# Step 1's pieces placed one step behind the blocks of full-float32 products

## The chip, the cores and the metric

The kernel runs on one core of one Trainium2 chip. Its time is the device time of one execution, in microseconds. Before the change three runs took 1006.72, 1007.61 and 1007.96 us, median 1007.61. The profile is one further execution.

The engines are PE (matrix products), PEld (the loading of its stationary operand), ACT, DVE and POOL (elementwise work) and SP, which issues nearly all DMAs. Each engine does its instructions in program order and waits on semaphores for the others.

## The reference

```python
X = np.fft.fft(x, axis=1)           # x: 8 x 3136 x 256
X = np.fft.fft(X, axis=2)
x = X.real.astype(np.float32)
mu = np.mean(x, axis=-1, keepdims=True)
var = np.mean((x - mu) ** 2, axis=-1, keepdims=True)
xn = (x - mu) / np.sqrt(var + 1e-06) * g_ln
ch = np.maximum(xn @ w_ch1, 0.0) @ w_ch2
return x + ch
```

A two-dimensional Fourier transform of each of eight batches, of which the real part is kept, then a layer norm, a two-layer network with ReLU (256 to 1024 to 256), and a residual sum.

## The kernel before, in words

**The Fourier transform along the sequence** is done in two steps, 3136 = 64 x 49. Step 1 is a transform of length 64, step 2 one of length 49 with the twiddles in its table. Only half of the tokens (1567 a batch, `REG`, and two single ones) go through the network's first product, since the others are their mirror images; the transform along the 256 features is folded into the first weights and, for the residual, into a table `ty_s`.

**Chunks and steps.** The tokens of all batches stand in 49 chunks of 256. The main loop runs over steps s; step s works on chunk s // 8 and on 128 of the 1024 inner features. In a step, PE does six products in `moe1_a` (L354, into a PSUM tile `ab`, two buffers) and, for the step three before, twelve in `moe2` (L404, into `acc`). They are float32 numbers split in a high and a low part, three passes for each product. ACT copies half of `ab` to `asb` (L359), DVE makes `h` of it (L360, L361), ACT rounds `h` to `h_hi` (L368) and DVE makes `h_lo` (L369). `moe1_b(s - 1)` comes ahead of `moe1_a(s)`, so on ACT and DVE h_hi and h_lo of a step stand ahead of asb and h of the next.

**Further work** is put into two lists by step: `late` (after `moe1_a`) and `after` (at the end of the step). The order within each engine is the order in which the program writes it.

- *Blocks.* At steps 5 mod 8 `step2` (L309, products in full float32, one or two groups of tokens; a step with two is called a double block here) and `residual` (L428, also full float32) make one block on PE. ACT copies the results at the same step (L330, L332), DVE makes the low part `ckl` one step later (L334). `residual_e` (ACT) and `residual_y` (DVE, L442 to L455) follow one to three steps behind, `std` (ACT, L460) at steps 1 mod 8, `inverse_std` (DVE, L467 to L471: a reciprocal and three small operations) at steps 2 mod 8, and `finish` (L477, L479) at 3 and 4 mod 8. For the first group of a batch, `step2` adds a product with `zmu` (L313).
- *Step 1's pieces.* Each batch has seven, `step1(b, i)`: three products of 512 columns (L262) at the end of a step d, into PSUM tile `y` (one buffer), which the second group of a double block uses too; ACT copies the result into `s1` (L265) and SP stores it (`store1`, L269). Ahead of it, POOL folds the input, `fold_zw` at d - 7 (L207, L208) and `fold_eo` at d - 6 (L213, L214), ACT rounds the fold, `fold_hi` at d - 4 (L219), and POOL makes its low part, `fold_lo` at d - 3 (L225). `load_x` of the next batch stands at d - 5. POOL does these in their order as soon as their data and buffers are there, so it often runs ahead of the steps.
- *Edge products.* `ends` (POOL, L190, L194) and `step1_ends` (PE, L237 to L241, then two copies on ACT, the second into the last column of `zmu`).
- *Relayout.* Two steps behind the last piece, SP reads the stored result back in another order (`relayout`, L276) for `step2`.

A batch b needs its relayout at step `need` = 8 * (b * REG // CW) - 3, the step of its block with the zmu product. These are the steps 45, 93, 141, 189, 237, 285 and 333 for batches 1 to 7. The pieces of batches 2 to 7 stand at need - 45, - 42, - 37, - 34, - 29, - 26 and - 21, so at 0 or 3 mod 8, and `fold_hi` at 4 or 7 mod 8.

Of the kernel before, what the change touches and what calls it, by code (L numbers as in the profile page):

```python
# [20 lines left out]
F32 = mybir.dt.float32  # L21
# [7 lines left out]
NB, N, D, FF = 8, 3136, 256, 1024  # L29
NV = 25  # L30
HALF = N // 2 + 1
REG = HALF - 2
CW = 256
# [9 lines left out]
KP = 8 * NS  # L43
# [103 lines left out]
def tile_kernel(ctx: ExitStack, tc: tile.TileContext, x, g_ln, w1, w2, tu, tab, tz, ty, tw, out):  # L147
    nc = tc.nc
    moving = ctx.enter_context(tc.tile_pool(name="moving", bufs=1))
    weights = ctx.enter_context(tc.tile_pool(name="weights", bufs=1))  # L150
    const = ctx.enter_context(tc.tile_pool(name="const", bufs=1))
# [14 lines left out]
    tz_s = const.tile([KP, 50], F32, name="tz_s")  # L166
# [3 lines left out]
    ty_s = const.tile([128, 2, 130], F32, name="ty_s")  # L170
    g_s = const.tile([128, 2], F32, name="g_s")
    xs = const.tile([128, NU, 4, D], F32, name="xs")
    zmu = const.tile([KP, 128], F32, name="zmu")
    masked = const.tile([128, KP], F32, name="masked")
    one = const.tile([128, 1], F32, name="one")
    neg = const.tile([128, 1], F32, name="neg")
# [51 lines left out]
    def alloc1(b):  # L228
        if b not in s1:
            s1[b] = work.tile([128, NS, 2, 128], F32, tag="s1", name=f"s1_{b}", bufs=1)  # L230
            scratch[b] = dram.tile([NS, 128, D], F32, tag="scratch", name=f"scratch{b}")

    def step1_ends(b, p0=0, p1=NS):
        alloc1(b)
        n = p1 - p0
        ps = psum.tile([128, 3, n], F32, tag="y" if b else "fft", name=f"pse{p0}_{b}")
        nc.tensor.matmul(ps[:, 0], tu_s[:, 0:128], e0c[b][:, p0:p1, 1], start=True, stop=True)  # L237
        nc.tensor.matmul(ps[:, 1], tu_s[:, 256:384], e0c[b][:, p0:p1, 0], start=False, stop=True,
                         skip_group_check=True)
        if p1 == NS:  # L240
            nc.tensor.matmul(ps[:KP, 2, 0:1], masked, one, start=False, stop=True,  # L241
                             skip_group_check=True)
        nc.scalar.copy(s1[b][:, p0:p1, :, 127], ps[:, 0:2].rearrange("p h s -> p s h"))
        if p1 == NS:
            nc.scalar.copy(zmu[:, 127:128], ps[:KP, 2, 0:1])

    def step1(b, i):
        alloc1(b)
# [36 lines left out]
    def first_token(m):  # L285
        b, j = divmod(m, 8)
        return b * REG + max(gb[2 * j] - 2, 0)
# [11 lines left out]
    def step2(m, part, of=None):  # L299

        b, j = divmod(m, 8)
        base, end = gb[2 * j], gb[2 * j + 2]
        if "m" in part:
            ps2[m] = psum.tile([128, 2, CW], F32, tag="y" if m in second else "fft", name=f"ps2_{m}")
        ps = ps2[m]
        for g in (2 * j, 2 * j + 1) if "m" in part else ():
            k0, k1 = gb[g], gb[g + 1]
            for h in range(2):
                nc.tensor.matmul(ps[:, h, k0 - base:k1 - base], s2[b][:KP, g, 128 * h:128 * h + 128],  # L309
                                 tab_s[:, h, k0:k1], start=(h == 0 and g == 2 * j), stop=True,  # L310
                                 skip_group_check=True)
            if g == 0:
                nc.tensor.matmul(ps[:, 1, 0:50], zmu, tz_s, start=False, stop=True,  # L313
                                 skip_group_check=True)
        if j == 0 and "f" in part:
            nc.scalar.copy(single[:, :, 2 * b:2 * b + 2], ps[:, :, 0:2])
        t, stop = first_token(m), b * REG + end - 2
        while t < stop:
            c = t // CW
            n = min(stop, c * CW + CW) - t  # L320
            if c not in chunk:
                parts = (weights.tile([128, 2, CKW - 32], F32, tag="ck", name=f"ck{c}", bufs=3),
                         moving.tile([128, 2, CKW], F32R, tag="ck_hi", name=f"ckh{c}", bufs=3),
                         moving.tile([128, 2, CKW], F32R, tag="ck_lo", name=f"ckl{c}", bufs=3))
                chunk[c] = tuple(p[:, :, :MAXW] for p in parts)
            full, hi, lo = (x[:, :, t - c * CW:t - c * CW + n] for x in chunk[c])
            p0 = t - b * REG + 2 - base
            src = ps[:, :, p0:p0 + n]
            if "h" in part and of in (None, c):
                nc.scalar.copy(hi, src)  # L330
            if "f" in part:
                nc.scalar.copy(full, src)  # L332
            if "l" in part and of in (None, c):
                nc.vector.tensor_tensor(out=lo, in0=src, in1=hi.bitcast(F32), op=ALU.subtract)  # L334
            t += n
# [272 lines left out]
    def add(s, fn, *args):  # L608

        after.setdefault(s, []).append((fn, args))  # L610

    def add_late(s, fn, *args):

        late.setdefault(s, []).append((fn, args))

    first = {}
    for m in range(3, 64):
        s = 8 * (first_token(m) // CW) - 3
# [3 lines left out]
    for s, ms in first.items():  # L622
        for m in ms:
            add(s, step2, m, "mhf")
        for m in ms:
            add_late(s + 1, step2, m, "l")
    for b in range(1, NB):
        need = 8 * (b * REG // CW) - 3
        at = [need - d for d in ((45, 42, 37, 34, 29, 26, 21) if b > 1 else
                                 (28, 25, 22, 19, 17, 14, 11))]  # L630
        ends_at = need - (46 if b > 1 else 30)
        add(ends_at - 7, ends, b)
        add(ends_at, step1_ends, b)
        for i, d in enumerate(at):
            d0, d = d, d - (b == 1)
            add(d - 7, fold_zw, b, i, nc.gpsimd)
            if b + 1 < NB:
                add(d - 5, load_x, b + 1, i)
            add(d - 6, fold_eo, b, i)
            add(d - 4, fold_hi, b, i)  # L640
            add(d - 3, fold_lo, b, i)
            add(d0, step1, b, i)
            add(d0, store1, b, i)
        add(at[-1] + 2, relayout, b)
    for c in range(LC):
        s = 8 * c + (5 if c > 1 else 6)
# [26 lines left out]
    with tc.manual_schedule(engines={E.PE, E.Activation, E.DVE, E.Pool}):  # L673
        with tc.manual_schedule(engines={E.SP}):
# [33 lines left out]
            nc.sync.dma_start(tab_s[:, :, :gb[4]], tab[:, :, :gb[4]])  # L708
            nc.sync.dma_start(tz_s, tz)
            step1_ends(0, 0, 6)  # L710
            for i in range(3):
                store1(0, i, nc.scalar if i % 2 else nc.gpsimd)
# [5 lines left out]
            step1(0, 4)  # L718
            finish_w1(0)
            step1_ends(0, 6, 10)  # L720
            store1(0, 3, nc.scalar)
            store1(0, 4, nc.gpsimd)
# [46 lines left out]
            convert_b("w2_1")  # L769
            warm_up(15, warm_h)  # L770
            step2(0, "m")
            step2(0, "hl")
            step2(1, "m")
# [72 lines left out]
```

## Time and profile before

| | |
|---|---|
| median of the three runs | 1007.61 us |
| the profiled execution | 1007.27 us |
| its span, from the first to the last instruction | 1005.5 us |
| PE's granted clock, mean | 1.000 |
| products L404 | 3 x 1568, mean 279 ns |
| products L354 | 3 x 768, mean 279 to 286 ns |
| pieces' products L262 | three for each of 49 pieces |
| copies L265 | 56, mean 585 ns |

PE's products are pipelined: each lasts 279 ns in the trace, and the next starts 113 to 118 ns behind it. The time of a product on PE is therefore read from start to start, not from its duration.

In the rows of a timeline the first column is the start in us from the span's start, the second the duration in us; behind a form in square brackets stand the engine's idle time before the instruction and what ended it. In the rows of waits stand the total in us, the number of times and the longest. In the rows of windows stand the window, its length, the busy time of the engine with the number of instructions that touch it, the granted clock, the DMA's busy share and GB/s.

The chain of work that ended last has PE for 88% of the span (L404 49%, L354 25%), DVE for 7% and ACT for 2%.

### The profile page before, as it was taken

To read this page: it belongs to the slowest core of one execution; us is meant where nothing else is said; L and a number is where in the kernel's file an instruction comes from. 1 tells how busy PE (TensorE), PEld (TensorE's weight loads), DVE (VectorE), ACT (ScalarE), POOL (GpSimd) and SP (SyncE) were. 2 spreads that over 40 slices of the span, in tenths; PEclk is the share of its full clock that TensorE was granted. 3 is DMA by queue.
4 is the path that set the end of the run, shared out by engine and by line. 5 is a ranking of instruction groups with operands and counts; after the bars stand their busy time and mean duration, and the time that the engine had idled before them with its cause. 6 is when DMAs were issued, how large, how long until landed. Compare 5 with 4: busy or idle time off the path is not lost.

```text
span 1005.5 us, 21770 instructions
## 1 busy us (share of the span) xinstructions
PE 995.1 (99%) x8289; PEld 973.7 (97%) x8289; DVE 812.3 (81%) x2190; ACT 540.1 (54%) x1416; POOL 243.9 (24%) x278
## 2 busy tenths in 40 slices
PE   9999999999999999999999999999999999999998
PEld 6799999999999999999999999999999999999998
DVE  7788887878787788878877887878788788887887
ACT  3655556554555555655456555555555554555553
POOL 2146414530153203440054401532034300000000
PEclk9999999999999999999999999999999999999999
DMA  9933243223122511333132232224101230100101
GB/s 346 266 141 126 85 143 110 86 84 108 62 95 85 157 44 53 103 120 105 44 111 101 74 106 75 84 96 126 55 32 44 74 105 23 43 22 22 43 22 43
DMA packets 41528, 92.10 MB, mean 92 GB/s; under 512 B 4176, under 2 KB 18704, under 8 KB 40528
## 3 DMA queue, kind: packets, MB, share of 16 engines
q1 hardware_dynamic: 40016, 88.87, 27.1%
q8 instruction: 66, 1.08, 0.5%
q0 software_dynamic: 320, 1.05, 0.3%
q10 hardware_dynamic: 1088, 0.79, 0.2%
q14 instruction: 38, 0.31, 0.1%
HBM read 50.32 MB, written 40.37 MB: 90 GB/s over the span
## 4 chain that ended last, share of the span: by engine, by line
PE 88%; DVE 7%; ACT 2%; DMA 2%; issue 1%; SPq 0%; ACTq 0%; DVEq 0%
PE acc L404 49%; PE ab L354 25%; PE ps L309 5%; PE psy L428 4%; PE ps L262 3%; DVE h_lo L369 2%; DVE h L360 1%; DVE h L361 1%; ACT h_hi L368 1%; PE ps L255 1%; PE ps L257 1%; DMA scratch<-s 1%; DMA s<-scratch 1%; DMA xs<-x 0%; DVE st L450 0%
## 5 line engine op out<-in xcount | busy, mean ns | idle before, releaser
L404 PE MATMUL acc<-w_hi,h_lo 128*128 128x256 f32 x1568 | 437.1, 279 | 0.2 <-DVE h_lo L369 0.2
L404 PE MATMUL acc<-w_hi,h_hi 128*128 128x256 f32 x1568 | 436.9, 279 | 0.0
L404 PE MATMUL acc<-w_lo,h_hi 128*128 128x256 f32 x1568 | 436.9, 279 | 0.0
L369 DVE SCALAR_TENSOR_TENSOR h_lo<-h,h_hi 128x512 fp32r<-128x512 f32 x392 | 285.9, 729 | 160.8 <-ACT h_hi L368 159.0
L368 ACT ACTIVATE h_hi<-h 128x512 fp32r<-128x512 f32 x392 | 250.1, 638 | 266.0 <-DVE h L361 265.5
L404 PEld LDWEIGHTS acc<-w_hi,h_hi 128*128 128x128 f32 x1568 | 296.7, 189 | 0.0
L404 PEld LDWEIGHTS acc<-w_lo,h_hi 128*128 128x128 f32 x1568 | 295.3, 188 | 0.0
L404 PEld LDWEIGHTS acc<-w_hi,h_lo 128*128 128x128 f32 x1568 | 294.6, 188 | 0.6 <-DVE h_lo L369 0.4
L354 PE MATMUL ab<-ckl,w_hi 128*128 128x256 f32 x768 | 219.9, 286 | 2.6 <-DVE h L361 2.5
L354 PE MATMUL ab<-ckh,w_lo 128*128 128x256 f32 x768 | 214.5, 279 | 0.5 <-ACT ckh L330 0.3
L354 PE MATMUL ab<-ckh,w_hi 128*128 128x256 f32 x768 | 214.1, 279 | 0.0
L225 POOL TENSOR_TENSOR fl<-f,fh 128x512 fp32r<-128x512 f32 x49 | 64.2, 1309 | 495.5 <-ACT fh L219 489.3
L360 DVE TENSOR_TENSOR h<-asb,ab 128x256 f32<-128x256 f32 x384 | 158.7, 413 | 1.5 <-ACT asb L359 1.5
L361 DVE TENSOR_TENSOR h<-asb,ab 128x256 f32<-128x256 f32 x384 | 158.8, 414 | 0.0
L354 PEld LDWEIGHTS ab<-ckl,w_hi 128*128 128x128 f32 x768 | 144.3, 188 | 6.5 <-issue 2.1
L359 ACT COPY asb<-ab 128x256 f32<-128x256 f32 x384 | 139.0, 362 | 17.6 <-PE ab L354 13.9
L354 PEld LDWEIGHTS ab<-ckh,w_lo 128*128 128x128 f32 x768 | 144.7, 188 | 3.1 <-ACT ckh L330 0.5
L354 PEld LDWEIGHTS ab<-ckh,w_hi 128*128 128x128 f32 x768 | 145.3, 189 | 0.0
L330 ACT CAST ckh<-ps 128x392 fp32r<-128x392 f32 (+49 forms) x112 | 39.8, 356 | 62.3 <-PE ps L309 62.1
L265 ACT COPY s<-ps 128x508 f32<-128x508 f32 x56 | 32.8, 585 | 71.9 <-PE ps L262 58.7
L309 PE MATMUL ps<-tab_s,s 112*128 112x98 f32 (+1 forms) x512 | 65.6, 273 | 0.6 <-DMA s<-scratch 0.6
L309 PEld LDWEIGHTS ps<-tab_s,s 112*128 112x128 f32 x512 | 61.9, 191 | 1.1 <-PE pw L670 1.1
(108 smaller groups left out, 964.8 us busy)
## 6 DMA issues: line engine op xcount, KB each, us to landing
xs<-x SPq DMA_DIRECT2D x56, 512.0 KB, 4.4
out<-o SPq DMA_DIRECT2D x96, 256.0 KB, 3.0
scratch<-s SPq DMA_DIRECT2D x49, 256.0 KB, 2.2
s<-scratch SPq DMA_DIRECT2D x7, 1792.0 KB, 9.7
w1p_all<-w SPq DMA_DIRECT2D x8, 512.0 KB, 8.7
scratch<-s POOLq DMA_DIRECT2D x4, 256.0 KB, 6.3
s<-scratch SPq DMA_DIRECT2D x2, 448.0 KB, 5.8
s<-scratch SPq DMA_DIRECT2D x1, 896.0 KB, 12.2
```

The costliest lines, as they stand in the source:

```text
L225: nc.gpsimd.tensor_tensor(out=lo, in0=f, in1=hi.bitcast(F32), op=ALU.subtract)
L265: nc.scalar.copy(s[:, :, :, :127], ps[:, :, :, :127])
L309: nc.tensor.matmul(ps[:, h, k0 - base:k1 - base], s2[b][:KP, g, 128 * h:128 * h + 128], tab_s[:, h, k0:k1], start=(h == 0 and g == 2 * j), ...
L330: nc.scalar.copy(hi, src)
L354: nc.tensor.matmul(pt, wt[wi][:, j, fs], ch[xi][:, j, :w], start=(n == 0), stop=(n == 2))
L359: nc.scalar.copy(asb[:, :w], pa)
L360: nc.vector.tensor_tensor(out=h[:, :w], in0=asb[:, :w], in1=pb, op=ALU.add)
L361: nc.vector.tensor_tensor(out=h[:, w:], in0=asb[:, :m], in1=pb[:, :m], op=ALU.subtract)
L368: nc.scalar.activation(h_hi, h, AF.Relu)
L369: nc.vector.scalar_tensor_tensor(out=h_lo, in0=h, scalar=0.0, in1=h_hi.bitcast(F32), op0=ALU.max, op1=ALU.subtract)
L404: nc.tensor.matmul(acc[c, i][:, side], hs[xi][:, h0:h0 + 128], ws[wi][:, f], start=(f == 0 and side == 0 and n == 0), stop=(f == 7 and n = ...
L428: nc.tensor.matmul(ps[:, j, :129 + j], ck[:, j], ty_s[:, j, :129 + j], start=(j == 0), stop=True, skip_group_check=True)
```

## The change

Batch 1 keeps its steps. For batches 2 to 7:

- Five of the seven pieces stand behind the blocks at need - 56, - 40, - 32, - 24 and - 16: one step behind a single block (6 mod 8), two behind a double one (7 mod 8). The other two stand in neighbouring steps, need - 46 and need - 45, behind the block with the zmu product of the batch before. What belongs to a piece (folds, loads, store) keeps its distance to it.
- The relayout keeps its two steps behind the last piece, so it comes at need - 13 or need - 12 instead of need - 19.
- `step1_ends` stands at need - 58 instead of need - 46, `ends` at need - 62 instead of need - 53.
- As the edge products of a batch now come before the zmu product of the batch ahead of it, `zmu` has two columns' worth, one for even and one for odd batches.

```diff
-    zmu = const.tile([KP, 128], F32, name="zmu")
+    zmu = const.tile([KP, 2, 128], F32, name="zmu")
...
-            nc.scalar.copy(zmu[:, 127:128], ps[:KP, 2, 0:1])
+            nc.scalar.copy(zmu[:, b % 2, 127:128], ps[:KP, 2, 0:1])
...
-                nc.tensor.matmul(ps[:, 1, 0:50], zmu, tz_s, start=False, stop=True,
+                nc.tensor.matmul(ps[:, 1, 0:50], zmu[:, b % 2], tz_s, start=False, stop=True,
...
+    def behind(s):
+
+        return s + 1 + (len(first[s]) > 1)
+
+    steps1 = {1: [17, 20, 23, 26, 28, 31, 34]}
+    for b in range(2, NB):
+        need = 8 * (b * REG // CW) - 3
+        steps1[b] = sorted([need - 46, need - 45] +
+                           [behind(need - d) for d in (56, 40, 32, 24, 16)])
     for b in range(1, NB):
         need = 8 * (b * REG // CW) - 3
-        at = [need - d for d in ((45, 42, 37, 34, 29, 26, 21) if b > 1 else
-                                 (28, 25, 22, 19, 17, 14, 11))]
-        ends_at = need - (46 if b > 1 else 30)
-        add(ends_at - 7, ends, b)
+        at = steps1[b]
+        ends_at = need - (58 if b > 1 else 30)
+        add(need - 62 if b > 1 else ends_at - 7, ends, b)
         add(ends_at, step1_ends, b)
```

`first[s]` is the list of the groups that `step2` does at step s; a double block has two.

## The prediction

> **What bounds the kernel now.** I read the page first, then the waits of PE, then PE's busy time in chosen stretches, last the timelines of single engines.
>
> ```profile
> PE 995.1 (99%) x8289; PEld 973.7 (97%) x8289; DVE 812.3 (81%) x2190; ACT 540.1 (54%) x1416; POOL 243.9 (24%) x278
> ```
> ```profile
> PE ab L354 <- DVE h L361: 2.5, 5, 0.8
> ...
> PE ps L262 <- DVE ckl L334: 1.1, 1, 1.1
> ```
>
> PE is busy for 99% of the span and hardly waits: the two rows (us, times, longest) are the only waits of the main loop that matter here. So time can go only where PE's products become quicker, and can come only from a wait that isn't there yet.
>
> Products do have two speeds. Five stretches (length, PE busy, instructions that touch it, granted clock): two of eight steps each, from the first product behind a block of full-float32 products to the next block; then three single steps.
>
> ```profile
> 469.85:486.89 17.04, 17.04 (x147) 1.00 0.06 21
> 488.60:505.02 16.42, 16.42 (x148) 1.00 0.10 36
> 414.39:416.51 2.12, 2.12 (x20) 1.00 0.00 0
> 421.30:423.34 2.04, 2.04 (x20) 1.00 0.00 0
> 424.04:426.16 2.12, 2.12 (x20) 1.00 0.19 65
> ```
> ```profile
> 416.51 0.39 PE L262 MATMUL ps<-fl,t_hi 128*128 128x512 f32 x1
> ...
> 423.34 0.39 PE L262 MATMUL ps<-fl,t_hi 128*128 128x512 f32 x1
> ```
>
> The same 144 products (18 a step) take 17.04 or 16.42 us, at the same full clock: a slow pace of 2.12 us a step and a fast one of 2.04, 0.62 / 8 = 0.078 apart. A pace holds until something other than L354 and L404 runs on PE. The last three rows stand around step 1's pieces (L262) at 416.51 and 423.34: a piece turns slow to fast, the next turns fast to slow. A block entered at the fast pace leaves the slow one; the block with the zmu product, and the edge products, leave the fast one. By these turns 24 of the 48 steps of a batch are slow now.
>
> **The change, part by part.**
>
> *Pace.* From batch 2 on a piece stands at the end of the first step behind a block (of the second, if the block is double), so a block's slow pace lasts one or two steps; the pair behind the zmu block has one slow step between. Per batch: five blocks without zmu, two of them double, and the pair: 5 + 2 + 1 = 8 slow steps. 16 of 48 turn fast; with the ends of the run 98 steps over six batches: 98 x 0.078 = **-7.6 us**. Products are neither added nor removed; batch 1 keeps its steps.
>
> *What a piece behind a block does to ACT and DVE.* Steps 5 mod 8 end with the block. After one, at the fast pace and without a piece, it goes today as follows (first products of steps 6, 3 and 4; then ACT; then DVE):
>
> ```profile
> 370.42 0.37 PE L354 MATMUL ab<-ckl,w_hi 128*128 128x256 f32 x1
> ...
> 380.72 0.28 PE L354 MATMUL ab<-ckl,w_hi 128*128 128x256 f32 x1
> ...
> 382.76 0.28 PE L354 MATMUL ab<-ckl,w_hi 128*128 128x256 f32 x1
> ```
> ```profile
> 372.73 0.63 ACT L368 ACTIVATE h_hi<-h 128x512 fp32r<-128x512 f32 x1
> ...
> 379.64 0.63 ACT L368 ACTIVATE h_hi<-h 128x512 fp32r<-128x512 f32 x1 [1.05 <-DVE h L361]
> 380.17 0.35 ACT L359 COPY asb<-ab 128x256 f32<-128x256 f32 x1
> ```
> ```profile
> 379.19 0.41 DVE L361 TENSOR_TENSOR h<-asb,ab 128x256 f32<-128x256 f32 x1
> ...
> 381.24 0.41 DVE L361 TENSOR_TENSOR h<-asb,ab 128x256 f32<-128x256 f32 x1
> 381.57 0.16 DVE L467 RECIPROCAL ve<-ve 128x2 f32<-128x2 f32 x1
> 381.76 0.16 DVE L468 SCALAR_TENSOR_TENSOR ve<-ve 128x2 f32<-128x2 f32 x1
> ```
>
> Step s+2 needs the PSUM buffer that DVE frees with h of step s. h of step 1 ends at 379.60, step 3 starts at 380.72: 1.12 us to spare; one step on 382.76 - 381.65 = 1.11. DVE's round (h, ACT's h_hi, h_lo, h) takes 381.24 - 379.19 = 2.05 us, no less than PE's fast step: what is lost there isn't won back before the next block.
>
> A piece's copy L265 stands on ACT ahead of the next h_hi:
>
> ```profile
> 437.12 0.28 PE L354 MATMUL ab<-ckl,w_hi 128*128 128x256 f32 x1
> ```
> ```profile
> 437.32 0.58 ACT L265 COPY s<-ps 128x508 f32<-128x508 f32 x1 [1.74 <-PE ps L262]
> 437.80 0.64 ACT L368 ACTIVATE h_hi<-h 128x512 fp32r<-128x512 f32 x1
> ```
>
> It starts 0.20 after the next step's first product, h_hi 0.48 later. With the piece at the end of step 6 (2.20 for that step, 0.70 for the piece: 417.21 less 416.51 in the same timeline), h_hi of step 6 starts 2.90 + 0.68 = 3.58 us after the step does, instead of 372.73 - 370.42 = 2.31. DVE is 1.27 late, PE 0.76. To spare at step 2: 1.11 - 1.27 + 0.76 = **0.60 us**. The same working gives 0.89 behind a double block (piece a step later, while DVE does its y work) and 1.38 behind the zmu block with its two pieces. No wait of PE by itself.
>
> *Where a piece's fold falls.* fold_hi is four steps ahead of the piece. For a piece at 6 mod 8 that is step 2; POOL's fold_lo follows at once, and zw and f of the next piece back to back. Just then DVE does inverse_std (L467 to L471): in the rows above fold_hi would start near 380.44, behind asb, POOL near 381.15 for 1.3 us, and L468 comes at 381.76. Batch 1 has this meeting now (POOL; DVE; PE):
>
> ```profile
> 105.57 1.30 POOL L225 TENSOR_TENSOR fl<-f,fh 128x512 fp32r<-128x512 f32 x1 [2.17 <-ACT fh L219]
> 106.83 0.73 POOL L213 TENSOR_TENSOR f<-zw 128x256 f32<-128x256 f32 x1
> 107.52 0.74 POOL L214 TENSOR_TENSOR f<-zw 128x256 f32<-128x256 f32 x1
> ```
> ```profile
> 105.20 0.41 DVE L361 TENSOR_TENSOR h<-asb,ab 128x256 f32<-128x256 f32 x1
> 105.53 0.16 DVE L467 RECIPROCAL ve<-ve 128x2 f32<-128x2 f32 x1
> 105.72 1.16 DVE L468 SCALAR_TENSOR_TENSOR ve<-ve 128x2 f32<-128x2 f32 x1
> 106.92 0.66 DVE L469 TENSOR_TENSOR ve<-ve 128x2 f32<-128x2 f32 x1
> 107.61 0.66 DVE L471 SCALAR_TENSOR_TENSOR r<-ve 128x2 f32<-128x2 f32 x1
> ...
> 109.13 0.41 DVE L361 TENSOR_TENSOR h<-asb,ab 128x256 f32<-128x256 f32 x1
> ```
> ```profile
> 109.68 0.36 PE L354 MATMUL ab<-ckl,w_hi 128*128 128x256 f32 x1 [0.63 <-DVE h L361]
> ```
>
> L468, L469 and L471 each end when a POOL operation does. From h to h 109.13 - 105.20 = 3.93 us pass instead of 2.05, 1.88 are lost, and PE waits until 0.14 after h. In the new places no L265 stands ahead of fold_hi, so POOL starts 0.48 earlier against DVE and L468 waits 0.5 less; but POOL's run goes on and reaches h_lo, which took 1.07 instead of 0.69 in such a place:
>
> ```profile
> 400.35 1.07 DVE L369 SCALAR_TENSOR_TENSOR h_lo<-h,h_hi 128x512 fp32r<-128x512 f32 x1 [0.70 <-ACT h_hi L368]
> ```
>
> Loss per meeting: 1.88 - 0.48 + 0.38 = 1.78; PE waits 1.78 - (spare - 0.15): 1.33, 1.04 or 0.55. The plan has 15 meetings, fold_hi at steps 58, 82, 114, 162, 298 behind single blocks, 106, 130, 154, 178, 210, 258 behind double ones, 50, 194, 242, 290 behind zmu blocks (a batch's last piece is left out: there POOL must first wait for x, and only fold_lo meets DVE): 6.65 + 6.24 + 2.20 = 15.1 us.
>
> The Trainium skill, page "SBUF — State Buffer", section "Who interferes with whom", speaks against the new places: a DVE instruction with two SBUF inputs and a GpSimd instruction that reads SBUF exclude each other for a whole instruction, one with at most one SBUF input doesn't contend. The rows agree (L360 and L361, which read PSUM, keep 0.41). By it h_lo could be held for a whole 0.74 operation, 15 x 0.36 = 5.4 us more than my sum.
>
> *The edge products* move to step 3 mod 8, in three of these cycles (82, 130, 178) between the meeting and PE's wait:
>
> ```profile
> 392.95 0.29 PE L237 MATMUL pse<-e0c,tu_s 128*128 128x14 f32 x2
> ...
> 393.51 0.36 PE L354 MATMUL ab<-ckl,w_hi 128*128 128x256 f32 x1
> ```
>
> They take 0.56 of PE's time here as there, but in these cycles that shortens the wait: 3 x 0.56 off, **+13.4 us** for the meetings. Bounds: 0, if POOL and DVE miss each other, to 15 x 1.88 = 28, with nothing to spare.
>
> *The rest, together.* The second zmu column costs nothing in the loop: ACT writes one column as before. The loads, stores and the relayout keep their order on SP; the relayout still has twelve steps, some 25 us, before the zmu block reads it; were that too little, PE would wait there. At a double block a piece takes the buffer y of the second product block, two steps behind it; that place is where the 1.1 us row comes from, in batch 1, where DVE was late. At 0 to 1.1 for eleven such pieces, 0 to 12 us, I take 0, since outside batch 1 DVE has no such delay ahead of it.
>
> Sum against the profiled execution of 1007.3 us: 1007.3 - 7.6 + 13.4 = 1013.1; the median of the runs is 0.3 above it: **1013.4 us**.
>
> **The rivals.**
> - *The pace alone: faster.* The meetings cost nothing, because the offset of fold_lo against inverse_std is another, or because there is more than 1.9 us to spare (from there on a meeting is free). For it: the spare is a difference of larger numbers. Against it: the offset is fixed by the chain h, h_hi, asb, fold_hi. 1007.6 - 7.6 = 1000.0, to 1004 with some waits. 25%.
> - *They cancel.* Half the price of the meetings: 1007.6 - 7.6 + 7 = 1007. 10%.
> - *The pace isn't turned there.* A piece one step behind a block, or a zmu block reached in another way, leaves the pace slow; the meetings stay: 1007.6 + 13.4 = 1021. Against it: pieces two steps behind a block turned it. 7%. The Trainium skill, page "TensorE: Matmul & The Clock Gate", section "Wait — 56ns, not 53.3ns?", has one warm start-to-start time, N / 2.4 plus about 2.5 ns, 109 ns for 256 columns, and so no second pace to win; this trace has two, 2.04 / 18 = 113 ns and 2.12 / 18 = 118 ns.
>
> **How the numbers follow.** The forecast has 58%, with 1008 to 1021 as its own range; with the faster rival the range is 998.5 to 1021. About 0.2%, 2 us, is what a measurement of this kernel can tell from no change. Slower: 58 + 7 less 3 for the forecast's low edge, 62%; faster 25 + 2 of the cancelling case, 27%; same 11%.
>
> **What would show it.** Waits of PE for h L361 at about 15 steps 5 mod 8, near 1 us each, with L468 to L471 long beside L225: the meetings are right. L468 at 0.16 throughout and no such wait: they are wrong, and the time is near 1000. Steps behind the pieces at 2.12: the turns are wrong.

## The result: slower by a fifth of a per cent, less than half of what was forecast

| | before | after |
|---|---|---|
| median | 1007.34 us (20 runs, 1006.43 to 1009.52) | 1009.85 us (20 runs, 1007.63 to 1011.55) |
| profiled execution, its span | 1007.27, 1005.5 us | 1010.0, 1008.2 us |

The ratio is 1.0021, with an interval of 1.0014 to 1.0028: slower by 2.5 us. The forecast was 1013.4 us, slower by 5.8 than the 1007.6 known then; the measured time lies in the forecast's own range of 1008 to 1021.

**The page of the changed kernel**, busy time, share of the span and instructions of each engine:

```profile
PE 993.7 (99%) x8289; PEld 969.7 (96%) x8289; DVE 833.4 (83%) x2190; ACT 534.6 (53%) x1416; POOL 240.2 (24%) x278
```

DVE is busy for 21 us more with the same instructions: something makes them longer. PE's busy time fell by 1.4 us while the span grew by 2.7, so PE now stands still for longer. The waits of PE (us in total, times, longest):

```profile
PE ab L354 <- DVE h L361: 6.4, 13, 0.8
...
PE ps L262 <- DVE ckl L334: 1.2, 1, 1.2
```

Before, the first row had five waits and 2.5 us, all ahead of step 35; the other eight are new. DVE's groups (busy us, mean ns), `inverse_std`'s three small operations first, then one of them before the change:

```profile
L468 DVE SCALAR_TENSOR_TENSOR ve<-ve 128x2 f32<-128x2 f32 (+1 forms) x49 | 19.1, 389 | 1.7
L469 DVE TENSOR_TENSOR ve<-ve 128x2 f32<-128x2 f32 (+1 forms) x49 | 16.4, 334 | 1.7
L471 DVE SCALAR_TENSOR_TENSOR r<-ve 128x2 f32<-128x2 f32 (+1 forms) x49 | 14.8, 303 | 1.7
```
```profile
L468 DVE SCALAR_TENSOR_TENSOR ve<-ve 128x2 f32<-128x2 f32 (+1 forms) x49 | 9.3, 189 | 1.7
```

So the meetings with POOL are there: L468 takes twice as long on average. The third thing to look at is the pace. Two stretches of 126 products each, from behind a piece to the next block, as windows of the changed kernel (length, PE busy, instructions that touch it, clock, DMA share, GB/s):

```profile
197.87:212.16 14.29, 14.29 (x127) 1.00 0.21 74
454.06:468.90 14.84, 14.84 (x127) 1.00 0.22 71
```

The first is what the change was to give, 113 ns a product. The second stands behind a piece of the same kind and is slow all the same, at 118.

**The account.** From step 35 to eight steps before the end, all products L354 and L404 of a trace were sorted by the time to the next such product: up to 115 ns is fast (mean 113.3), 116 to 122 slow (mean 117.8). What a longer one exceeds 115 ns by is counted as waiting; the start of a block's followers is kept apart.

| | stretch, us | fast | slow | waiting, us |
|---|---|---|---|---|
| before | 851.98 | 2887 | 3251 | 0.0 |
| after | 854.46 | 4029 | 2080 | 7.1 |

1171 products left the slow pace: 1171 x 4.4 ns = -5.2 us. The waiting is +7.1 us. (The view has 4.2 us in eight waits there. It begins a wait at the last product's end, 0.28 us behind its start, where the next product was due after 0.113; it has no waits shorter than that difference; and the second product behind a wait is late too, some 0.193 us behind the first.) The rest, +0.6, lies in and around the blocks; 0.4 of it is at the residual products (L428) of step 37. The sum, +2.5 us, is the result.

### The profile page after: what moved, and what is told of

It is laid out like the page before. It is cut to its first block, busy times and chain, and to the rows that moved or that the text cites. A ratio compares the mean times of both kernels' runs of the same rounds, so it can differ in the third digit from the quotient of the medians.

```text
span 1008.2 us, 21760 instructions
## 1 busy us (share of the span) xinstructions
PE 993.7 (99%) x8289; PEld 969.7 (96%) x8289; DVE 833.4 (83%) x2190; ACT 534.6 (53%) x1416; POOL 240.2 (24%) x278
## 4 chain that ended last, share of the span: by engine, by line
PE 80%; DVE 13%; ACT 3%; DMA 2%; issue 2%; SPq 0%; ACTq 0%; DVEq 0%
PE acc L404 43%; PE ab L354 22%; PE ps L309 5%; DVE h_lo L369 4%; PE psy L428 4%; PE ps L262 3%; DVE h L361 2%; DVE h L360 2%; ACT h_hi L368 2%; DVE st L450 1%; DVE ve L468 1%; DVE ve L469 1%; DMA scratch<-s 1%; ACT s L265 1%; PE ps L255 1%
## 5 line engine op out<-in xcount | busy, mean ns | idle before, releaser
L404 PE MATMUL acc<-w_hi,h_lo 128*128 128x256 f32 x1568 | 435.7, 278 | 0.1
L404 PE MATMUL acc<-w_lo,h_hi 128*128 128x256 f32 x1568 | 435.5, 278 | 0.0
L404 PE MATMUL acc<-w_hi,h_hi 128*128 128x256 f32 x1568 | 435.5, 278 | 0.0
L368 ACT ACTIVATE h_hi<-h 128x512 fp32r<-128x512 f32 x392 | 249.7, 637 | 322.2 <-DVE h L361 322.1
L404 PEld LDWEIGHTS acc<-w_hi,h_hi 128*128 128x128 f32 x1568 | 295.6, 189 | 0.0
L404 PEld LDWEIGHTS acc<-w_lo,h_hi 128*128 128x128 f32 x1568 | 295.1, 188 | 0.0
L404 PEld LDWEIGHTS acc<-w_hi,h_lo 128*128 128x128 f32 x1568 | 294.6, 188 | 0.4 <-DVE h_lo L369 0.3
L354 PE MATMUL ab<-ckl,w_hi 128*128 128x256 f32 x768 | 220.4, 287 | 6.5 <-DVE h L361 6.4
L354 PE MATMUL ab<-ckh,w_lo 128*128 128x256 f32 x768 | 213.9, 278 | 0.5 <-ACT ckh L330 0.4
L354 PE MATMUL ab<-ckh,w_hi 128*128 128x256 f32 x768 | 213.4, 278 | 0.0
L225 POOL TENSOR_TENSOR fl<-f,fh 128x512 fp32r<-128x512 f32 x49 | 64.1, 1307 | 527.1 <-ACT fh L219 478.4
L354 PEld LDWEIGHTS ab<-ckl,w_hi 128*128 128x128 f32 x768 | 144.3, 188 | 12.5 <-issue 7.6
L354 PEld LDWEIGHTS ab<-ckh,w_lo 128*128 128x128 f32 x768 | 144.7, 188 | 3.1 <-ACT ckh L330 0.5
L354 PEld LDWEIGHTS ab<-ckh,w_hi 128*128 128x128 f32 x768 | 144.8, 189 | 0.0
L359 ACT COPY asb<-ab 128x256 f32<-128x256 f32 x384 | 138.2, 360 | 10.8 <-PE ab L354 9.2
L265 ACT COPY s<-ps 128x508 f32<-128x508 f32 x56 | 32.8, 585 | 64.3 <-PE ps L262 50.5
```

Source lines behind the costliest of these rows:

```text
L225: nc.gpsimd.tensor_tensor(out=lo, in0=f, in1=hi.bitcast(F32), op=ALU.subtract)
L265: nc.scalar.copy(s[:, :, :, :127], ps[:, :, :, :127])
L354: nc.tensor.matmul(pt, wt[wi][:, j, fs], ch[xi][:, j, :w], start=(n == 0), stop=(n == 2))
L359: nc.scalar.copy(asb[:, :w], pa)
L368: nc.scalar.activation(h_hi, h, AF.Relu)
L404: nc.tensor.matmul(acc[c, i][:, side], hs[xi][:, h0:h0 + 128], ws[wi][:, f], start=(f == 0 and side == 0 and n == 0), stop=(f == 7 and n = ...
```

## The experiments

Each was run beside the kernel before on the same chip; that kernel's median was 1007.25 for the first four, 1007.93 for the next three and 1007.48 for the last two. Three theories were at stake: that the waits come from the meetings of POOL with `inverse_std`; that it takes the piece's copy L265 ahead of h_hi as well; and that the pace is what the pieces' places were to win.

**1. The changed kernel without its meetings.** For pieces at 6 mod 8 both folds come one step later.

```diff
-            add(d - 4, fold_hi, b, i)
-            add(d - 3, fold_lo, b, i)
+            later = b > 1 and d % 8 == 6
+            add(d - 4 + later, fold_hi, b, i)
+            add(d - 3 + later, fold_lo, b, i)
```

> The changed kernel, with fold_hi and fold_lo of the pieces at steps 6 mod 8 (batches 2 to 7) one step later, so that POOL's fold_lo no longer runs beside DVE's inverse_std; nothing else moves. Theory A (the meeting of the two makes PE's waits, and the waits also upset the pace): L468, L469 and L471 fall back to 0.16 us in the loop, PE's waits for h fall from 6.4 us (13) to the 2.5 us (5) of the kernel of before, the slow products behind step 35 fall from 2080 to about 1460, and the time is 7.6 us below the kernel of before: about 0.9925 of it. Rival B (the spare of 0.6 us is the cause, and any run of POOL or ACT work at that place uses it up): waits stay near 6 us, ratio 1.00 to 1.002. Rival C (the pace isn't turned reliably in the new places, waits or not): waits go, but slow products stay near 2000, ratio about 0.996.

Measured: 1001.91 us, ratio 0.9943 [0.9931, 0.9956]; the stretch 846.05 us, 1621 slow products, no waiting for h. Its timelines around one `inverse_std` (DVE, then POOL; start, duration):

```profile
324.74 0.16 DVE L467 RECIPROCAL ve<-ve 128x2 f32<-128x2 f32 x1
324.93 0.16 DVE L468 SCALAR_TENSOR_TENSOR ve<-ve 128x2 f32<-128x2 f32 x1
325.12 0.16 DVE L469 TENSOR_TENSOR ve<-ve 128x2 f32<-128x2 f32 x1
325.32 0.16 DVE L471 SCALAR_TENSOR_TENSOR r<-ve 128x2 f32<-128x2 f32 x1
```
```profile
326.35 1.30 POOL L225 TENSOR_TENSOR fl<-f,fh 128x512 fp32r<-128x512 f32 x1 [14.10 <-ACT fh L219]
```

L225 starts 1.03 us behind L471's start, when L471 has long ended, and L468 keeps 0.16. So it is Theory A of the expectation; of its 0.9925 some 1.8 us are missing: 1621 products are slow where 1460 were expected (126 of them behind one piece, see experiment 6), and PE waits in a new place. One step's difference in the place of the folds is worth 1009.85 - 1001.91 = 7.9 us. The waits of this kernel show what took their place:

```profile
PE ab L354 <- DVE h L361: 1.5, 3, 0.7
...
PE psy L428 <- DVE o L479: 1.0, 1, 1.0
```

At step 37, where the fold now meets `finish`, PE waits once for L479.

**2. The changed kernel with its meetings, the copy out of the way.** For batches 2 to 7 L265 comes behind h_hi and asb of the next step, the store a step later.

```diff
+            if b > 1:
+                add_late(d0 + 1, step1_copy, b, i)
-            add(d0, store1, b, i)
+            add(d0 + (b > 1), store1, b, i)
```

`step1_copy` is L265 by itself, on the PSUM tile that `step1` keeps for it.

> The changed kernel, with ACT's copy of a piece (L265, batches 2 to 7) moved behind h_hi and asb of the next step, and its store with it; folds stay, so fold_lo still meets inverse_std. Theory A with my sum (a wait is the 1.4 us lost in a meeting less what DVE has to spare, and the copy ahead of h_hi takes 1.27 us of the spare): spare at step 2 rises from 0.6 to about 1.9 us, L468 stays long (0.67 us) in 15 cycles, but PE's waits fall to those of before, slow products to about 1460, ratio about 0.9925. Rival (the meeting costs PE whatever there is to spare, or the copy doesn't matter): waits stay near 6 us, ratio 1.002.

Measured: 1003.12 us, ratio 0.9964 [0.9952, 0.9977]; waiting 1.0 us, at four places, 1937 slow products. This kernel.py has nine lines more above these places, so L265 is L274 here, L368 is L377, L359 is L368 and L468 is L477. The copy behind h_hi and asb, and DVE's group:

```profile
176.75 0.63 ACT L377 ACTIVATE h_hi<-h 128x512 fp32r<-128x512 f32 x1
178.24 0.37 ACT L368 COPY asb<-ab 128x256 f32<-128x256 f32 x1 [0.85 <-PE ab L363]
178.51 0.59 ACT L274 COPY s<-ps 128x508 f32<-128x508 f32 x1
```
```profile
L477 DVE SCALAR_TENSOR_TENSOR ve<-ve 128x2 f32<-128x2 f32 (+1 forms) x49 | 20.3, 415 | 1.7
```

So the meetings are there and cost little waiting: it takes both, the loss in the meeting and the copy ahead of h_hi. The spare grew by less than expected: behind single blocks it is 1.26 us, where 1.9 was expected and the changed kernel has 0.6. A loss of 1.28 less (1.26 - 0.15) leaves 0.17, and the four waits are 0.16 to 0.19 long, all behind single blocks. The ratio of 0.9925 was missed as well: the slow products fell by only 143, and the median lies above that of the first experiment. Behind three of the four waits the products are slow, and the next piece then leaves PE at the slow pace for 126 products: short waits cost pace too.

**3. Both.** The edits of 1 and 2 in one kernel.

> Both edits at once. Theory A: either alone already frees PE, so both together give no more than the better one, ratio 0.992 to 0.993. If the two faults add up (each leaves some wait), both together are clearly faster than each alone, by 2 us or more.

Measured: 1000.86 us, ratio 0.9937 [0.9923, 0.995]; 1604 slow products, no waiting. Beside the first experiment this is no difference that can be told: without the meetings the copy's place is free.

**4. The kernel before, with meetings.** For the pieces at 0 mod 8 both folds come two steps earlier, so that POOL meets `inverse_std` with no piece and no copy behind a block.

```diff
-            add(d - 4, fold_hi, b, i)
-            add(d - 3, fold_lo, b, i)
+            sooner = 2 * (b > 1 and d % 8 == 0)
+            add(d - 4 - sooner, fold_hi, b, i)
+            add(d - 3 - sooner, fold_lo, b, i)
```

> The kernel of before, with fold_hi and fold_lo of its pieces at steps 0 mod 8 two steps earlier (batches 2 to 7), so that 24 meetings of fold_lo with inverse_std come about in the old places. By my sum: to spare at step 2 in these cycles 1.1, 1.3, 2.0 and 2.0 us, so a meeting that loses 1.4 us costs 0.44, 0.24, 0 and 0: 6 x 0.7 = 4 us, ratio 1.004, with about 12 waits of PE. Rival (a meeting costs PE its whole loss): 24 x 1.4 = 34 us, ratio 1.03. Rival (a meeting alone is harmless, only the new places make it cost): no new wait, ratio 1.000.

Measured: 1010.78 us, ratio 1.0035 [1.0021, 1.0048]; waiting 2.5 us at five places (0.33 us three times, 0.56 twice), 3277 slow products. Its group of L468 and its waits:

```profile
L468 DVE SCALAR_TENSOR_TENSOR ve<-ve 128x2 f32<-128x2 f32 (+1 forms) x49 | 21.6, 442 | 1.7
```
```profile
PE ab L354 <- DVE h L361: 3.4, 10, 0.8
```

The meetings slow the kernel before as well, by about the ratio expected; but only five places wait, less than half of the 12 expected, though L468 is even longer on average than in the changed kernel (442 against 389 ns). With the 1.1 to 2.0 us to spare that the expectation names, instead of 0.6, most meetings are covered.

**5. The pace alone.** The changed kernel with its five pieces five steps behind their blocks, the edge products and `ends` four steps later than in the changed kernel.

```diff
-                            [behind(need - d) for d in (56, 40, 32, 24, 16)])
+                            [need - d + 5 for d in (56, 40, 32, 24, 16)])
```

> The changed kernel, with the five pieces of a batch that stand behind blocks put five steps behind them (2 mod 8), their folds with them, so fold_lo falls at 7 mod 8 and doesn't meet inverse_std; the edge products stand at need - 54, their ends at need - 58, so that they stay behind the last piece of the batch before. Same products, no meeting, no piece behind a block. Pace theory (a block leaves PE slow until a piece turns it): 26 slow steps of 48, about 3500 slow products behind step 35 against 1621 in the run with the later fold, 1900 x 4.4 ns = 8 us lost against that run, ratio to the kernel of before about 1.001. Rival (what the run with the later fold gained comes from elsewhere, say shorter waits or queues): ratio about 0.994 as there, and slow products near 1600.

Measured: 1009.73 us, ratio 1.0019 [1.001, 1.0028]; the stretch 854.38 us, 3763 slow products, no waiting. The same work in the same number of products takes 8.3 us more in the stretch than in the first experiment, and (3763 - 1621) x 4.4 ns = 9.4 us is what the pace gives, less the one wait of the first. Two windows: five steps (90 products) from a block to a piece, and three (54) from that piece on:

```profile
313.13:323.82 10.69, 10.69 (x94) 1.00 0.14 47
324.52:330.65 6.13, 6.13 (x55) 1.00 0.24 87
```

10.69 / 90 = 119 ns (the first gap behind a block, 0.20 us, is in it), 6.13 / 54 = 113.5: the block is left at the slow pace, the piece turns it. One thing was not expected, once in each batch: edge products that PE reaches at the slow pace are left at the slow pace, and the piece behind them doesn't turn it. That is why there are more slow products here than expected.

**6. The edge products of batch 2.** In the first experiment 126 products are slow behind the first piece of batch 2, which stands behind edge products that PE reaches slow. Here that piece and those edge products come later, with the folds of 1.

```diff
+    steps1[2] = [47, 48, 50] + steps1[2][3:]
-        ends_at = need - (58 if b > 1 else 30)
-        add(need - 62 if b > 1 else ends_at - 7, ends, b)
+        ends_at = need - (58 if b > 2 else 47 if b > 1 else 30)
+        add(need - 62 if b > 2 else ends_at - 7, ends, b)
```

> The run with the later fold, with batch 2's first piece and edge products at steps 50 and 47 instead of 38 and 35, nothing else. Expected: the wait of the residual products at step 37 (1.2 us) goes, slow products stay at about 1620, as the stretch behind step 37 is slow either way: 1.2 us below the run with the later fold, ratio about 0.993. Rival (that wait is made up for later): no difference.

Measured: 1004.17 us, ratio 0.9959 [0.9944, 0.9974]: a miss, not better than the first experiment. The waits of PE say why:

```profile
PE ab L354 <- DVE h L361: 3.0, 7, 0.7
...
PE pse L237 <- DVE ckl L334: 1.1, 1, 1.1
```

The wait at step 37 is gone, as expected. But the edge products now wait 1.1 us for the PSUM tile that they share with a block's results, and three steps later PE waits 0.5 us for h. 63 products more than in the first experiment are slow.

**7. That, and the pieces behind single blocks in mid-step.** A piece at 6 mod 8 stands behind the six products L354 of its step instead of at its end, so that only those six stay slow. The edits of 6, and:

```diff
-            add(d0, step1, b, i)
+            if later:
+                mids.append((d0, b, i))
+            else:
+                add(d0, step1, b, i)
...
+    for d, b, i in mids:
+        add_late(d, step1, b, i)
```

> A try at the best version: the run with the later fold, with batch 2's first piece and edge products back behind the zmu block (steps 50 and 47 instead of 38 and 35), and the pieces behind single blocks put into the middle of the step, after moe1_a, instead of its end. A single block's slow pace then lasts 6 products instead of 18 (about 20 x 12 fewer slow products, 1.0 us), the copy L265 comes ahead of h_hi by 0.5 us less wait; the wait of the residual products for finish at step 37 (1.2 us) goes too. Expected 2 to 3 us below the run with the later fold, ratio 0.991 to 0.992. If DVE or ACT is now what limits, the gain is under 1 us.

Measured: 1002.43 us, ratio 0.9946 [0.9933, 0.9958]; 1448 slow products, 236 fewer than in experiment 6; waiting for h 0.6 us. A miss too, for the same waits.

**8. Mid-step alone.** The edits of 1 and the `mids` of 7; batch 2 keeps its steps, and its first piece (step 38) its folds.

```diff
-            later = b > 1 and d % 8 == 6
+            later = b > 1 and d % 8 == 6 and d != 38
```

> The run with the later fold, without the move of batch 2's first piece and edge products that made waits of its own in the two runs before; batch 2's first piece keeps its early fold, and the pieces behind single blocks (all but that one) stand in the middle of their step. From the product counts of the two runs before (1684 slow with the piece at the step's end, 1448 in its middle): about 1390 slow products instead of 1621, 1.0 us less, and 0.8 us less wait at step 37 if the fold's delay made it. Expected 1 to 2 us below the run with the later fold, ratio 0.992 to 0.994. Rival (ACT's or DVE's order in the middle of a step costs what the pace brings): no difference to the run with the later fold.

Measured: 998.68 us, ratio 0.9915 [0.9902, 0.9928]; the stretch 843.01 us, 1221 slow products, no waiting. It beats the kernel before by 8.8 us and, by the two ratios, the changed one by 10.7. Windows behind one block, in the first experiment (a whole slow step, then 126 products) and here (six slow products, then 138):

```profile
312.32:314.52 2.20, 2.20 (x21) 1.00 0.00 0
315.22:329.51 14.29, 14.29 (x127) 1.00 0.23 75
```
```profile
309.15:309.94 0.79, 0.79 (x10) 1.00 0.00 0
310.64:326.29 15.65, 15.65 (x140) 1.00 0.21 69
```

138 products in 15.65 us are 113.4 ns each. Against the first experiment there are 400 slow products fewer (1.8 us), and the wait of 1.0 us at step 37 is gone: 2.8 of the 3.0 us between the stretches.

Not all of the 400 are the work of the mid-step pieces. Behind step 46 the two kernels have 1201 and 1428 slow products, 227 fewer, about the 20 x 12 expected. The other 173 (0.8 us) lie in steps 35 to 45, where the edge products are here reached at the fast pace, and the piece behind the next block then turns PE to fast instead of leaving it slow. That goes back to a wait of PE at step 29, ahead of everything that the edit moves: the products behind it are slow here and fast in the first experiment. Why is not known; as far as the traces show, this part of the gain is luck.

**9. The first experiment again**, beside 8.

> The run with the later fold once more, unchanged, so that it stands beside the one with the pieces in the middle on the same chip: ratio 0.9943 within 0.0015.

Measured: 1001.07 us, ratio 0.9938 [0.9926, 0.995]; 1606 slow products. It repeats the first. Against it experiment 8 is 2.4 us faster by the medians; the intervals of the two ratios just meet at 0.993, so the gain of the mid-step pieces rests as much on the count behind step 46, 1201 slow products against 1428 both times, which is 1.0 us. The wait at step 37 is 0.4 us in this run and 1.0 in the first.

## Why it came out at less than half of the forecast

**Right: where and why PE waits.** The forecast had h_hi of step 6 start 3.58 us after that step, behind the piece's copy. ACT in the changed kernel, behind the block whose followers start at 175.09:

```profile
178.19 0.58 ACT L265 COPY s<-ps 128x508 f32<-128x508 f32 x1 [0.77 <-PE ps L262]
178.67 0.63 ACT L368 ACTIVATE h_hi<-h 128x512 fp32r<-128x512 f32 x1
```

178.67 - 175.09 = 3.58. The time to spare at step 2, measured in the same way, is 0.62 us behind single blocks, 0.89 behind double ones and 1.37 behind zmu blocks (forecast 0.60, 0.89, 1.38). All 15 meetings took place, and 13 of them left a wait.

**Wrong: the loss per meeting, 1.78 us.** It is 1.27. The meeting behind that block, POOL, DVE and PE:

```profile
187.06 1.30 POOL L225 TENSOR_TENSOR fl<-f,fh 128x512 fp32r<-128x512 f32 x1 [15.32 <-ACT fh L219]
188.31 0.73 POOL L207 TENSOR_TENSOR zw<-xs 128x256 f32<-128x256 f32 x1
189.00 0.64 POOL L208 TENSOR_TENSOR zw<-xs 128x256 f32<-128x256 f32 x1
189.72 1.13 POOL L213 TENSOR_TENSOR f<-zw 128x256 f32<-128x256 f32 x1
```
```profile
185.12 0.41 DVE L361 TENSOR_TENSOR h<-asb,ab 128x256 f32<-128x256 f32 x1
...
187.18 0.41 DVE L361 TENSOR_TENSOR h<-asb,ab 128x256 f32<-128x256 f32 x1
187.51 0.16 DVE L467 RECIPROCAL ve<-ve 128x2 f32<-128x2 f32 x1
187.70 0.67 DVE L468 SCALAR_TENSOR_TENSOR ve<-ve 128x2 f32<-128x2 f32 x1
188.41 0.65 DVE L469 TENSOR_TENSOR ve<-ve 128x2 f32<-128x2 f32 x1
189.09 0.56 DVE L471 SCALAR_TENSOR_TENSOR r<-ve 128x2 f32<-128x2 f32 x1
189.58 0.68 DVE L369 SCALAR_TENSOR_TENSOR h_lo<-h,h_hi 128x512 fp32r<-128x512 f32 x1
...
190.51 0.41 DVE L361 TENSOR_TENSOR h<-asb,ab 128x256 f32<-128x256 f32 x1
```
```profile
191.06 0.36 PE L354 MATMUL ab<-ckl,w_hi 128*128 128x256 f32 x1 [0.65 <-DVE h L361]
```

From h to h 190.51 - 187.18 = 3.33 us pass, the round before took 187.18 - 185.12 = 2.06: 1.27 lost. The forecast's terms were 1.88 - 0.48 + 0.38. The -0.48 holds: L468 takes 0.67 where batch 1 had 1.16, 0.49 less. The +0.38 for h_lo fell: h_lo keeps 0.68. L471 ends when POOL's L208 does, h_lo starts at 189.58, POOL's next, L213, at 189.72, and it is POOL that takes 1.13 instead of 0.74. L471 itself took 0.56, 0.10 less than in batch 1. So 1.88 - 0.49 - 0.10 = 1.29, within 0.02 of the 1.27 measured (the 15 meetings lose 1.27 to 1.30), and the forecast charged DVE for an operation that POOL paid for.

The Trainium skill, page "SBUF — State Buffer", section "Who interferes with whom", has the rule that bears on this: the shared ports are an exclusive lock, and issue order decides who blocks. The rows agree, and by the order of the two starts the 5.4 us more, which the forecast had worked out by that page beside its sum, fall as well.

With 1.27 in place of 1.78 the forecast's own formula, loss - (spare - 0.15), gives 0.82 behind single blocks, 0.53 behind double ones and 0.04 behind zmu blocks. Measured were 0.82 (four times), 0.56 (four times) and 0.07 to 0.08 (four times). In the three cycles with edge products the 0.56 us that they take covers the wait of two wholly and leaves 0.15 of the third, where 0.26 would be left by the formula. One more wait, 0.07, stands at 584.5 us, at a batch's last piece, which the forecast had left out. The second products behind the 14 waits, each 0.08 us late, add 1.1 us, a term that the forecast did not have. All together 7.1 us in place of 13.4.

**Wrong: the pace, -7.6 us.** It brought 5.2. The places of the turns were right: without waits for h (first experiment) 1630 products leave the slow pace, 7.2 us, where 98 steps of 18, or 1764, had been forecast. What the forecast didn't see is that a wait of PE can turn the pace as well. PE's timeline around one wait:

```profile
447.31 0.36 PE L354 MATMUL ab<-ckl,w_hi 128*128 128x256 f32 x1 [0.66 <-DVE h L361]
...
449.51 1.03 PE L309 MATMUL ps<-tab_s,s 112*128 112x98 f32 x8
...
451.22 0.36 PE L354 MATMUL ab<-ckl,w_hi 128*128 128x256 f32 x1
...
453.37 0.39 PE L262 MATMUL ps<-fl,t_hi 128*128 128x512 f32 x1
```

Up to the wait the products are fast; the 16 behind it, up to the block, are slow. The block is then entered slow and left fast from its fourth product on, and the piece at 453.37, meant to turn slow to fast, turns fast to slow. What follows is the window 454.06 to 468.90 above: 126 slow products. Of the 14 waits, seven are followed by slow products up to the block, seven by products at the fast pace after at most four. At three of the first seven (446, 584 and 683 us) the block is then left fast, and the piece behind it turns to slow for 126, 90 and 126 products; at the other four the block is left slow, and only the products behind the wait are lost. Seven times 16 and these 342 are 454, about the 459 by which 1171 falls short of 1630. The forecast treated waits and pace as two terms of a sum; they are coupled. Experiment 2 against 3 shows it with the folds alone changed: 1.0 us of waits goes with 1937 slow products, none with 1604.

**The rivals.** "The pace alone" is the first experiment, 1001.91: its time is right, its condition isn't met by the change. "They cancel" had half the price of the meetings, and that is what they cost, 7.1; its 1007 was missed because the pace gave less as well. "The pace isn't turned there" is refuted by the window at 197.87. Both terms were sized too large; as their signs differ, the sum is off by 3.6 us only, where the meetings alone are off by 6.3.

**Open.** Why a wait turns the pace in seven cases and not in the other seven was not found, nor why the block behind it is then left fast at three places and slow at four; the length of the wait doesn't decide it (0.93, 0.19 and 0.67 us from product to product at the three). That the wait is the cause rests on its place in the trace and on experiments 1 to 3, not on a wait made by itself. The kernel before gives a hint that the forecast's turns left out: behind step 35, eight of nine blocks that PE reached at the slow pace left by the block ahead were left fast (the one at 486.89 us is in the windows of the forecast), and all twelve reached at the slow pace left by a piece were left slow. So there seem to be two kinds of the slow pace, and a wait may leave either; no run shows more than that.

## What to carry to other kernels

Look at the gap from product to product, not at PE's busy share: a kernel with PE at 99% had 14 us in two paces of the same products at the same clock. When work is moved for one engine's sake, list what its helpers on the other engines will meet in the new place: here the helper's start relative to three operations of 0.16 us decided the sign. And before charging both engines for a meeting, see which one starts first: here only the other paid.

## What the hardware showed that was not expected

- Products of 256 columns run at 113.3 or 117.8 ns from start to start, at the same granted clock, and a pace holds for up to 144 products (the window 469.85 to 486.89 of the kernel before). A piece of three products mostly turns it, a block without the zmu product that is reached at the fast pace leaves the slow one (but for one place in experiment 2), and, which was new, a wait of PE turns it in seven of 14 cases of the changed kernel, one of 0.07 us among them.
- Edge products reached at the slow pace leave it slow, and the next piece then doesn't turn it (experiment 5, once a batch): there is more to the state than the pace that one sees.
- The operations of 0.16 us on DVE that read two tiles in SBUF (L468, L469, L471) take 0.56 to 0.67 beside one of 0.6 to 1.3 us on POOL, and the first of them 1.16 in batch 1; the reciprocal L467, with one input, keeps 0.16 beside L225. Where DVE's starts first it keeps its time (h_lo, 0.68), and POOL's L213 takes 1.13 instead of 0.74.
